# Attention and GLU layer on one core: DMA transposes, LN2 arithmetic on GpSimd, VectorE's exponential tiles planned ahead, and a 512-query chunk split in two

## The chip, the cores and the metric

The kernel runs on one NeuronCore of a Trainium2 chip. Times are device microseconds of that core for one launch, lower being better; the figure of a kernel is the median of its runs. The engines are named as in the profile: PE is TensorE (PEld its weight loads), ACT is ScalarE, DVE is VectorE, POOL is GpSimd, SP is SyncE, which here only issues DMAs. [...]

## The reference

One transformer layer over 2048 tokens of width 640, with 32 heads of 20 and a gated FFN of width 1728, all in bf16:

```python
def _A_ref(x, wqkv, wo):                       # B, S, D = 1, 2048, 640; H = 32, Dh = 20
    qkv = (x @ wqkv).reshape(B, S, 3, H, Dh).transpose(2, 0, 3, 1, 4)
    q, k, v = qkv[0], qkv[1], qkv[2]
    scores = jnp.einsum("bhqd,bhkd->bhqk", q, k) * (Dh ** -0.5)
    p = _softmax(scores, axis=-1)
    o = jnp.einsum("bhqk,bhkd->bhqd", p, v)
    return o.transpose(0, 2, 1, 3).reshape(B, S, D) @ wo

def _B_ref(x, w_gate, w_up, w_down):
    return (_gelu(x @ w_gate) * (x @ w_up)) @ w_down

h  = x + _A_ref(_layernorm(x), A_wqkv, A_wo)
h2 = h + _B_ref(_layernorm(h), B_w_gate, B_w_up, B_w_down)
```

## The kernel before

The program is written as a list of operations (`op`), each with its engine, an estimated duration, a priority (a lower number goes first) and the data that it reads and writes. `Sched.schedule` plays these operations against a small cost model: at every moment each engine takes the ready operation of the best priority for which a PSUM bank is free. The order that comes out is written as a fixed instruction stream for every engine, with semaphore waits. On the chip each engine therefore works strictly in the planned order, and an instruction that is later than planned holds up what the plan put behind it.

The queries are cut in chunks (`SIZES`), seven of them: 512, 512, 256, 256, 256, 128 and 128 rows. They are called chunk 0 to chunk 6 here; by rows, they begin at 0, 512, 1024, 1280, 1536, 1792 and 1920. A chunk is attended in slots of 512 columns (`slots`): one group of four heads times 512 queries, or two groups times 256, or four times 128. There are 32 slots, each with 64 tiles of 128 keys by 512 columns. The score matmuls of a tile (L850) go into PSUM, and the exponential comes next.

Most exponentials run on ACT, in units of three tiles and two tiles in turn (1536 and 1024 columns, banks 0 to 2 and 3 to 4), written to `pts` or to `pts2`, which the profile shows as part of `rege`. Eight tiles of every slot (two in the first) are computed by DVE with integer arithmetic instead (`d_exp`: one read of PSUM per tile at L810, then seven steps on each pair of tiles). The list `dtile` says beside which unit a DVE tile is put; `D_FIRST` and `D_SPAN` spread them over the slot. The product with V (PV, into bank 6) takes DVE tiles at the earliest `D_LAG` = 8 units after they were begun. The last PV of a slot takes all that are left:

```python
while final and d_done:
```

After each slot `epilogue` copies bank 6 to `osb` on DVE, transposes it on PE (L957), and divides into `o_nat` (L966). After a chunk's last slot `post` does the rest. For each tile of 128 rows: `o_nat` is transposed to `oT` on PE (`transposes`, L562) and evicted by DVE (L571), multiplied with `wo` (L614), and added on DVE to the x rows in `h_sb` (L999), which `prefetch` fetched on SP's queue; then come the statistics. For the chunk: `ln_rsqrt` computes the inverse deviation of the second layernorm (LN2) in some 14 small DVE instructions. For each tile again: the normalised row block `xn_t` is written on DVE and transposed to `hnT` (the same buffer as `oT`). Then the FFN: gate matmuls (L1027), copies by DVE (L1056), GELU on ACT in pieces of up to 2048 columns, up matmuls (L1027), products on DVE (L1067), down matmuls (L1078), the last add (L1082) and the output DMA. GELU and the exponential need different tables on ACT; all GELU pieces of a chunk are run together. All of this is background work at priority `P_BG`, between the score matmuls (`P_QK`) and PV (`P_PV`) of the following chunks, in banks 7 and 5.

The last chunk (`tail=True`) has no attention beside it; there the evictions of transposes and the GELU are ACT's, and the square root is too.

Where a chunk's rows lie in `h_sb`, `hnT` and `ha_f` is set by `base`: a chunk of 512 takes all four places of 128 rows; a smaller one takes places 0 and 1, or 2 and 3, by whether its number is even or odd:

```python
return 2 * (c % 2) if CHUNKS[c][1] < 512 else 0
```

PE runs padding matmuls (on `zer` and on `kt_all`) where the plan would leave it idle, so that its clock stays up.

## Time and profile before

| | |
|---|---|
| median of 4 runs | 938.71 us (938.24 to 941.03) |
| the profiled execution, own time | 938.1 us |
| its span (first to last instruction) | 936.4 us |
| granted TensorE clock | 1.00 |
| busy: PE, DVE, ACT, POOL | 857.6, 828.4, 883.5, 12.8 us |
| first exponential begins, last one ends | 35.1, 892.9 us |
| ACT_TABLE_LOAD, all | 14 of 1.28 us |

The profile is of one execution. "Busy" is time in which an engine had an instruction under way; instructions overlap, so the mean duration of one times their number can be more than the busy time. A matmul's end is modelled. The names `rege` and `regw` are two large buffers out of which `h_sb`, `hnT`, `ha_f`, `pts2`, the FFN weights and others are carved; L339 is the line of the helper that records most operations. Attention, by the copies to `osb`, ends at 246.7 us for chunk 0, and then at about 454, 563, 671, 781, 837 and 893.

### The profile page before, as it was taken

The numbers are of one execution on the slowest core, as the hardware profiler recorded it, in microseconds if no ns is written. First come the engines' busy times: TensorE is split into PE (matmuls) and PEld (weight loads), VectorE is DVE, ScalarE is ACT, GpSimd is POOL, SyncE is SP. The second block draws the span as 40 slices with busy tenths as digits, with TensorE's granted clock in tenths as the row PEclk, the third lists the DMA queues.
The fourth block names the chain that finished last, engine by engine and source line by source line (L and its number), as shares of the span: only waits on it lengthen the run. The fifth ranks groups of instructions, "written<-read, shape, count | busy, mean of one in ns | idle before, by whom it ended". The sixth has DMA issues, their size and how long they took to land.

```text
span 936.4 us, 23514 instructions
## 1 busy us (share of the span) xinstructions
PE 857.6 (92%) x10297; PEld 365.1 (39%) x10297; DVE 828.4 (88%) x1807; ACT 883.5 (94%) x799; POOL 12.8 (1%) x33
## 2 busy tenths in 40 slices
PE   3998999999998999998898998999999899999998
PEld 2432222222232222332243333344434546566577
DVE  8859999999899988987799999798999989989953
ACT  7899999999999999999999999999999999999931
POOL 5000000000000000000000000000000000000000
PEclk9999999999999999999999999999999999999999
DMA  7301010322630000001000000000100000000000
GB/s 255 97 19 41 20 49 18 92 62 66 212 110 1 1 2 1 8 15 36 1 2 2 2 1 1 2 2 29 30 2 1 2 27 7 2 17 10 3 22 16
DMA packets 22046, 30.12 MB, mean 32 GB/s; under 512 B 1964, under 2 KB 19464, under 8 KB 21944
## 3 DMA queue, kind: packets, MB, share of 16 engines
q1 hardware_dynamic: 21944, 28.63, 10.0%
q8 instruction: 80, 1.31, 0.6%
q14 instruction: 22, 0.18, 0.1%
HBM read 20.12 MB, written 8.09 MB: 30 GB/s over the span
## 4 chain that ended last, share of the span: by engine, by line
ACT 77%; PE 14%; DVE 8%; issue 1%; DVEq 0%
ACT pts L339 50%; ACT rege L339 26%; PE ps L1027 4%; PE ps L614 3%; PE ps L850 2%; PE ps L1078 2%; PE ps L339 2%; DVE rege L339 2%; DVE qt_all L339 2%; ACT L339 1%; DVE stats L339 1%; DVE rege L810 1%; PE ps L562 1%; DVE qt_all L810 0%; DVE kt_all L339 0%
## 5 line engine op out<-in xcount | busy, mean ns | idle before, releaser
L339 ACT ACTIVATE pts<-ps 128x1536 bf16<-128x1536 f32 x480 | 574.0, 1383 | 6.1 <-PE ps L850 4.3
L850 PE MATMUL ps<-qt_all,kt_all 32*128 32x256 bf16 (+2 forms) x3584 | 303.6, 289 | 42.5 <-ACT pts L339 27.8
L339 ACT ACTIVATE rege<-ps 128x1536 bf16<-128x1536 f32 x239 | 300.7, 1384 | 3.1 <-PE ps L339 3.1
L850 PEld LDWEIGHTS ps<-qt_all,kt_all 32*128 32x128 bf16 x3584 | 95.8, 92 | 275.9 <-ACT pts L339 163.3
L339 DVE TENSOR_TENSOR qt_all<-qt_all 128x1024 bf16<-128x1024 bf16 (+1 forms) x240 | 164.1, 684 | 3.2
L1027 PE MATMUL ps<-rege,regw 128*128 128x256 bf16 (+2 forms) x980 | 152.8, 290 | 9.5 <-ACT rege L339 4.3
L339 PE MATMUL ps<-pts,v_all 128*21 128x256 bf16 (+2 forms) x2098 | 138.8, 290 | 0.5 <-DVE rege L339 0.5
L810 DVE TENSOR_SCALAR rege<-ps 128x512 int16<-128x512 f32 x154 | 105.3, 684 | 27.4 <-PE ps L850 26.5
L339 DVE TENSOR_SCALAR qt_all<-qt_all 128x1024 bf16<-128x1024 int16 (+1 forms) x288 | 115.6, 418 | 2.0
L339 PE MATMUL ps<-rege,v_all 128*21 128x256 bf16 (+2 forms) x1294 | 113.3, 292 | 0.0
L1027 PEld LDWEIGHTS ps<-rege,regw 128*128 128x128 bf16 x980 | 72.8, 97 | 63.5 <-issue 21.2
L614 PE MATMUL ps<-regw 128*128 128x512 bf16 (+1 forms) x360 | 86.3, 349 | 2.0 <-DVE v_all L747 0.7
L1078 PE MATMUL ps<-regw,rege 128*128 128x320 bf16 x448 | 78.0, 301 | 1.9 <-DVE rege L1067 0.8
L810 DVE TENSOR_SCALAR qt_all<-ps 128x512 int16<-128x512 f32 x96 | 65.6, 685 | 3.1 <-PE ps L850 2.2
L339 DVE TENSOR_SCALAR rege<-rege 128x1024 int16<-128x1024 int16 (+2 forms) x166 | 67.1, 420 | 1.1
L339 DVE TENSOR_TENSOR rege<-rege 128x1024 bf16<-128x1024 bf16 (+3 forms) x103 | 65.5, 643 | 0.9
L339 PE MATMUL ps<-kt_all,zer 128*32 128x512 bf16 x740 | 64.8, 385 | 0.0
L339 PEld LDWEIGHTS ps<-pts,v_all 128*21 128x21 bf16 x2098 | 50.2, 91 | 37.2 <-issue 30.8
L1078 PEld LDWEIGHTS ps<-regw,rege 128*128 128x128 bf16 x448 | 36.9, 98 | 32.6 <-issue 15.2
L339 PEld LDWEIGHTS ps<-rege,v_all 128*21 128x21 bf16 x1294 | 41.1, 91 | 19.7 <-issue 13.8
L614 PEld LDWEIGHTS ps<-regw 128*128 128x128 bf16 x360 | 28.4, 98 | 44.7 <-issue 20.2
L1067 DVE TENSOR_TENSOR rege<-rege,ps 128x512 bf16<-128x512 bf16 (+1 forms) x53 | 35.8, 678 | 10.5 <-PE ps L1027 9.7
(92 smaller groups left out, 595.3 us busy)
## 6 DMA issues: line engine op xcount, KB each, us to landing
rege<-in_A_x_dram SPq DMA_DIRECT2D x6, 640.0 KB, 5.1
q_rows<-regw SPq DMA_DIRECT2D x20, 128.0 KB, 1.7
out_dram<-rege SPq DMA_DIRECT2D x16, 160.0 KB, 2.1
regw<-in_B_w_gate_dram SPq DMA_DIRECT2D x1, 2160.0 KB, 12.4
regw<-in_B_w_up_dram SPq DMA_DIRECT2D x1, 2160.0 KB, 17.5
regw<-in_B_w_down_dram SPq DMA_DIRECT2D x1, 2080.0 KB, 22.6
kt_all<-k_rows SPq DMA_DIRECT2D x12, 160.0 KB
qt_all<-q_rows SPq DMA_DIRECT2D x12, 160.0 KB
```

Source lines behind the costliest of these rows:

```text
L339: return lambda eng: getattr(eng, method)(*args, **kwargs)
L562: op("pe", lambda eng, a=a: eng.transpose(bank16(bk, D)[:, 128 * a:128 * a + 128], src[:, a * 128:(a + 1) * 128], ident[:]), 0.055, prio, ...
L614: yield op("pe", lambda eng, l=l, r=r, k=k: eng.matmul(bank(bk, n), l, r, start=(k == 0), stop=(k == len(steps) - 1)), c_mm(n), prio, mode ...
L810: d_ops.append(op("dve", lambda eng: eng.tensor_scalar(v[:, 512 * h:512 * h + 512], bank(b), EXP_MUL, -32000.0, ALU.mult, ALU.max), c_dve( ...
L850: return lambda eng: eng.matmul(out()[:, kk * nq:(kk + 1) * nq], kt_all[32 * j:32 * j + 32, g, kt * 128:(kt + 1) * 128], qt_all[32 * j:32 ...
L1027: op("pe", lambda eng, a=a, f=f, fi=fi: eng.matmul(bank(bk)[:, fi * nq:(fi + 1) * nq], w[:, a, F0[f]:F0[f] + 128], hnT[:, a, 128 * tb:128 ...
L1067: hdone.append(op("dve", lambda eng, bu=bu, fv=fv, w=w: eng.tensor_tensor(fv, fv, bank(bu, w), ALU.mult), c_dve(w), p, reads=[ku, ("ha", k ...
L1078: op("pe", lambda eng, f=f, o=o, hf=hf, bk=bk: eng.matmul(bank(bk, 320), ha_f[:, o:o + 128], wd[:, f, hf * 320:(hf + 1) * 320], start=(f = ...
```

## The change

It has four parts.

- `SIZES` becomes 512, five of 256, and two of 128: the rows 512 to 1023 are two chunks of 256. `base` now counts the chunks of 256 to choose the half, and the last 128 rows take place 3, beside the 128 rows before them in place 2. `ha_f` is divided in quarters to fit, each x fetch has a semaphore of its own, and the wo matmuls wait for the x rows.
- In every chunk but the last, the transposes to `hnT` are done by DMAs issued by SP, and so are those to `oT` in every chunk but the first and the last.
- `ln_rsqrt` of every chunk but the last runs on POOL, but for its reciprocal, which stays on DVE. [...]The work up to xn and its transposes gets the priority `P_LN` = 2.5, ahead of `P_BG` = 3.
- DVE's tiles are first spread over 20 units, not 16, and then each is moved up by as many as `D_LEAD` = 8 units, into the slot before where need be. A DVE tile is taken by a PV of its own slot alone, and one that has waited `D_HOLD` = 4 units beyond its lag gets matmuls of its own in the next PV.

```diff
-SIZES = (512, 512, 256, 256, 256, 128, 128)
+SIZES = (512, 256, 256, 256, 256, 256, 128, 128)
-D_FIRST, D_SPAN = 1, 16
+D_FIRST, D_SPAN, D_LEAD, D_HOLD = 1, 20, 8, 4
-P_QK, P_PV, P_PRO, P_EPI, P_BG = 0, 1, 1.5, 2, 3
+P_QK, P_PV, P_PRO, P_EPI, P_LN, P_BG = 0, 1, 1.5, 2, 2.5, 3
...
-            d = lambda fn, r, w: op("dve", fn, 0.17, prio, reads=r, writes=w)
+            v = lambda fn, r, w: op("dve", fn, 0.17, prio, reads=r, writes=w)
+            d = v if table or sqrt else lambda fn, r, w: op(POOL, fn, 0.25, prio, reads=r, writes=w)
...
-            d(I("tensor_scalar", b.bitcast(I32), a.bitcast(I32), 1, None, ALU.logical_shift_right), ["nw0"], ["nw1"])
-            d(I("tensor_scalar", y.bitcast(I32), b.bitcast(I32), -1.0, RSQRT_MAGIC, ALU.mult, ALU.add), ["nw1"], rk)
+            d(I("tensor_scalar", y.bitcast(I32), a.bitcast(I32), -0.5, RSQRT_MAGIC, ALU.mult, ALU.add), ["nw0"], rk)
             for _ in range(2):
                 d(I("tensor_tensor", b, y, y, ALU.mult), rk, ["nw1"])
-                d(I("scalar_tensor_tensor", out=b, in0=b, scalar=-0.5, in1=a, op0=ALU.mult, op1=ALU.mult),
-                  ["nw0", "nw1"], ["nw1"])
-                d(I("scalar_tensor_tensor", out=y, in0=b, scalar=1.5, in1=y, op0=ALU.add, op1=ALU.mult),
-                  ["nw1"] + rk, rk)
+                d(I("tensor_tensor", b, b, a, ALU.mult), ["nw0", "nw1"], ["nw1"])
+                d(I("tensor_scalar", b, b, -0.5, 1.5, ALU.mult, ALU.add), ["nw1"], ["nw1"])
+                d(I("tensor_tensor", y, y, b, ALU.mult), ["nw1"] + rk, rk)
             d(I("tensor_tensor", sd16[:, t0:t0 + n], a, y, ALU.mult), ["nw0"] + rk, [ks])
-            d(I("reciprocal", y, sd16[:, t0:t0 + n]), [ks], rk)
+            v(I("reciprocal", y, sd16[:, t0:t0 + n]), [ks], rk)
...
+        def dma_transposes(src, rkeys, dst, wkey, after=()):
+            op("sp", I("dma_start_transpose", dst, src), 1.25, P_EPI, reads=rkeys, writes=[wkey], sem=f"xp{wkey[1]}", lat=2.0, after=after)
...
+        dtile = [None] * len(units)
+        u = 0
+        for n, x in dplan:
+            u = max(n - D_LEAD, u, D_FIRST, chunk_u[1] if slots[x[0]][0] == 1 else 0)
+            dtile[u] = x
+            u += 1
...
-                        if u - x_unit[x[2]] >= D_LAG and x[2][3] not in [y[2][3] for y in have]:
+                        if u - x_unit[x[2]] >= D_LAG and x[2][0] == s_ and x[2][3] not in [y[2][3] for y in have]:
                             have.append(x)
                             d_done.remove(x)
-                while final and d_done:
+                if any(x[2][0] == s_ and u - x_unit[x[2]] >= D_LAG + D_HOLD for x in d_done):
                     have = []
...
         def base(c):
-            return 2 * (c % 2) if CHUNKS[c][1] < 512 else 0
+            n = CHUNKS[c][1]
+            if n == 512:
+                return 0
+            half = sum(1 for _, m in CHUNKS[:c] if m == 256) % 2
+            return 2 * half + (n == 128 and CHUNKS[c - 1][1] == 128)
...
-            p = P_EPI if tail else P_BG
+            p = P_EPI if tail else P_LN
...
-                transposes(o_nat[:, tt, :], [("on", g, tt) for g in range(NG)], oT[:, :, tt * 128:(tt + 1) * 128],
-                           ("hnT", tt), banks, P_EPI, ev, after=first)
+                if tail or c == 0:
+                    transposes(o_nat[:, tt, :], [("on", g, tt) for g in range(NG)], oT[:, :, tt * 128:(tt + 1) * 128],
+                               ("hnT", tt), banks, P_EPI, "act" if tail else "dve", after=first)
+                else:
+                    dma_transposes(o_nat[:, tt, :], [("on", g, tt) for g in range(NG)], oT[:, :, tt * 128:(tt + 1) * 128],
+                                   ("hnT", tt), after=first)
...
-                                              for a in range(NA)], [("hnT", tt), "wo"], p))
+                                              for a in range(NA)], [("hnT", tt), "wo"], p, after=(sc.lw[("h", tt, hf)],)))
...
+                if tail:
+                    transposes(xn_t[:, t % 2, :], [("xn", t % 2)], hnT[:, :, tt * 128:(tt + 1) * 128], ("hnT", tt),
+                               banks, p, "act", after=first)
+                else:
+                    dma_transposes(xn_t[:, t % 2, :], [("xn", t % 2)], hnT[:, :, tt * 128:(tt + 1) * 128], ("hnT", tt),
+                                   after=first)
```

## The prediction

> **What bounds the kernel now.** First the page: busy shares, ACT's busy tenths in 40 slices, the chain that ended last.

> ```profile
> PE 857.6 (92%) x10297; PEld 365.1 (39%) x10297; DVE 828.4 (88%) x1807; ACT 883.5 (94%) x799; POOL 12.8 (1%) x33
> ACT  7899999999999999999999999999999999999931
> ...
> ACT 77%; PE 14%; DVE 8%; issue 1%; DVEq 0%
> ```

> ACT is full but for two slices at each end; POOL does nothing after its first memsets. Next the waits: who waited, for whom, us in total, times, longest.

> ```profile
> PEld ps L850 <- ACT pts L339: 163.3, 399, 1.1
> ...
> DVE rege L810 <- PE ps L850: 26.5, 29, 3.5
> ...
> ACT rege L339 <- PE ps L339: 3.1, 2, 1.6
> ...
> ACT pts L339 <- PE ps L339: 1.5, 3, 0.6
> ```

> The score matmuls wait for ACT 399 times, 0.41 us each; ACT hardly waits. In the chain an exponential of 1536 columns and one of 1024 take 2.26 us together, so the 719 take 812 of the 858 us between 35.1 and 892.9. Ten table loads take 13, the GELUs 23; what is left, some 10, is stalls and hand-overs.

> The end is another matter. The last exponential ends at 892.9, the span at 936.4. Timelines of ACT, SP, DVE and PE (start, us, instruction, count, idle before):

> ```profile
> 891.40 1.45 ACT L339 ACTIVATE rege<-ps 128x1536 bf16<-128x1536 f32 x1
> ...
> 904.19 0.34 SPq L339 DMA_DIRECT2D rege<-in_A_x_dram  x1
> ...
> 906.51 0.89 DVE L999 TENSOR_TENSOR rege<-ps,rege 128x320 bf16<-128x320 f32 x2 [0.45 <-DMA rege<-in_A_x_dram]
> ...
> 900.08 1.52 PE L614 MATMUL ps<-wo,rege 128*128 128x320 bf16 x10
> 901.44 6.00 PE L1078 MATMUL ps<-regw,rege 128*128 128x320 bf16 x43
> ...
> 912.01 8.93 PE L1027 MATMUL ps<-rege,regw 128*128 128x128 bf16 x157
> 920.78 3.97 PE L1078 MATMUL ps<-regw,rege 128*128 128x320 bf16 x28
> 924.58 4.52 PE L1027 MATMUL ps<-rege,regw 128*128 128x128 bf16 x78
> 929.62 3.98 PE L1078 MATMUL ps<-regw,rege 128*128 128x320 bf16 x28 [0.52 <-DVE rege L1046]
> ```

> Three chunks' FFN lie in these 43.5 us. The 56 down matmuls up to 907.4 belong to rows 1536-1791, attended by 781; of the 280 gate and up matmuls of 128 columns half, and 28 of the later down matmuls, belong to rows 1792-1919, attended by 837. Only the rest is the last chunk's. And the last chunk's residual add, whose matmuls end at 901.6, waits for its x rows till 906.5: their place in `h_sb` was only freed at 903.7.

> The cause of the lateness is upstream. By the timelines of o_nat, wo and xn_t, chunk 2 (rows 1024-1279) is attended by 563, but its x is fetched at 666.7, when the 512-row chunk 1 leaves `h_sb`, and its first gate matmul starts at 700; rows 1536-1791 need from 781 to 858. Their LN2 instructions run last in priority between DVE's exponential steps (rows 1280-1535 have their wo matmuls before 700 and their xn_t after 730).

> [...]

> **The change part by part.**

> *Split.* No exponential is added: 8 DVE tiles of 64 per slot stay (the last one now falls in unit 19 of 22). One chunk more means one more exp-GELU-exp switch: two loads at 1.30 us (889.18 to the next instruction at 890.48), **+2.6 us on ACT**. GELU columns are the same. PE: 140 matmuls of 512 columns (26 in 5.80 us, 0.223 each, 31.2) become 280 of 256 (13 in 1.59 us, 0.122 each, 34.2): +3 us, under PE's waits for ACT. DVE: two o_nat writes (0.313) for one (0.480) eight times, +1.2. SP: one x fetch more, 0.39.

> *DMA transposes.* 26 of them: one for each of chunk 0's 4 tiles, two for each of 11 others. They take off PE 130 transposes (10 in 0.73 us: 9.5 us) and off DVE 26 evictions at 0.48, 12.5 us; both are beside ACT. They add 26 issues on SP (the planner's 1.25 us each, 33 in all), waiting for o_nat or xn_t; x fetches and outputs queue behind, and SP's own waits show room (398.3 us for DVE's final adds alone). Landing is unknown: the nearest rows (160 KB out 2.1 us, x 2.3) and the planner's 1.25+2.0=3.25 below[...]. I take 3.25; PE, in order, stops if it is more.

> *LN2 on POOL.* 14 small instructions a chunk, 7 chunks. Bounds from POOL's rows: 0.10 us (1x1 memset) to 0.35 (128x160 select). I take 0.30, twice DVE's 0.155: 4.2 us a chunk, against the planner's 0.25 plus about 0.09 of hand-over each, 4.7. DVE loses 13 a chunk, 78 at 0.155, 12 us. [...]nothing on the path while DVE has 108 us idle. The reciprocal on DVE now waits for POOL; exponential steps, FFN evictions and osb copies queue behind it, and PE waits for those banks.

> *Priorities and places.* LN2 and wo now go ahead of FFN work, and 256-row chunks alternate halves of the buffers. Chunk 1's first half can start its FFN when chunk 0's is done (430) instead of after 468, so the backlog is gone before rows 1024-1279 come. Rows 1536-1791 should have gates near 800, not 858, and be done near 870 (chunk 2 needs 65 us, 700 to 765). Rows 1792-1919 follow with gate, GELU and up before 893: their GELU moves off the tail onto ACT, **+4.3** (two switches 2.6, 1.70 for 1792 columns). The last 128 rows get a quarter of their own, so their x is there early.

> *DVE tiles ahead.* Up to 8 units earlier, so the last PV of a slot has fewer left-over quads. Four stalls of ACT end with such a PV (at 92.3, 143.6, 195.3, 323.9: 0.57+1.46+0.38+1.63=4.0). I take **-3.0**; bounds 0 and -7.2, ACT's idle in all stages.

> *The sum.* Last exponential: 892.9+2.6+4.3-3.0=896.8. Tail with the last chunk alone: to the end of wo 8.7 (as now), add 0.5, statistics 0.7, to xn 2.5 (909.07 to 911.59), transposes 1.2, 140 gate and up matmuls at 57 ns 8.0, down 4.0, wait 0.5, last add and output 2.8 (933.6 to 936.4): 28.9. I add 1.0 for the GELU hand-over and 1.0 for what is left of rows 1792-1919: 30.9. Span 927.7, plus the 1.7 between span and own time (938.1): 929.4, or -8.7. The median is 938.7: **930.0 us**.

> **Rivals.**

> *Slower: late DMA transposes.* For: the planner puts their readers on PE as soon as its own figure lets it, and nothing in this trace backs 3.25. Against: 160 KB lands in 2.1 to 2.3. They come in 13 groups; each that lands late by x stops PE, and ACT by x-0.41. [...]It decides at 8.7/13+0.41=1.1 us late, 4.3 from issue to landing. A late POOL chain does the same through the reciprocal: one DVE instruction of 0.68 waited for at every step is 9.5 us a chunk; beyond the 8 units of lag that cover it, a few us, about 945.

> *Little gain.* The backlog stays because DVE (102 of 110 us busy in the stage from 671) limits it: only the wait for x goes, 901.6 to 906.5. 938.7-4.9+2.6=936.4.

> *The FFN of rows 1792-1919 stays in the tail.* Then ACT ends at 892.5, and 12 us of PE work meets 8.8 us of holes in the last chunk's chain: 929 to 931, the same answer.

> *More.* All stalls vanish (4.2 more) and nothing is left of the older rows: 925; with a faster LN2 chain in the tail 922.

> *Not ahead after all.* A tile moved ahead needs bank 7 or 5, which FFN chains hold: -3.0 is lost, 933.

> **How the numbers follow.** The forecast with its neighbours (928 to 933) 0.55, more 0.12, little gain 0.09, the slower rivals 0.20, cancelling ends near the present time 0.04. Within 0.2% (about what a measurement can tell) is 936.8 to 940.6: I put 0.05 there, 0.75 faster, 0.20 slower. The likeliest case's own range is 924 to 935; 8 in 10 need part of the slower case: 917 to 946.

> **What would show it.** Right: fourteen table loads (ten now) between 35 us and the last exponential, ACT idle under 5 us there, the last exponential at 894 to 898, no down matmuls of rows 1536-1791 after it, the last x fetch long before it, L1027 at 128 columns in the tail nearer 140 than 280. Wrong: PE waiting for DMA of oT, hnT or the xn transposes, over 0.5 us each; DVE's reciprocal waiting for POOL; ACT idle over 15 us in attention; or a tail still over 40 us.

## The result, and the profile after

| | before | changed |
|---|---|---|
| median | 938.58 us (937.8 to 941.03, 46 runs) | 935.59 us (928.14 to 941.89, 28 runs) |
| ratio to before | | 0.9971, 95% interval 0.9958 to 0.9984 |
| mean granted TensorE clock, by run | 0.998 to 1.000 | 0.982 to 1.000 |
| profiled execution: span | 936.4 us | 937.5 us, at clock 0.985 |
| last exponential ends, and the tail (from there to the end of the span) | 892.8, 43.6 us | 907.5, 30.0 us |

The change is faster by 0.3%, 3.0 us where 8.7 were forecast. (Three runs of the kernels below, two of "no split" and one of "PE transposes", took over 1.5% longer than the fastest of their kernel and are left out of every figure.) The spread is the first clue: the kernel before repeats within 3 us, the changed one ranges over 14. Over its 28 runs the span follows the clock: a straight line gives 927.6 us plus 0.75 us for each microsecond of clock lost (1 minus the mean clock, times the span), with a correlation of 0.985. The two runs at full clock have spans of 926.4 and 926.9, where 927.7 was forecast.

The page of the changed kernel, profiled at clock 0.985: busy time, ACT's busy tenths, the granted clock, and the chain that ended last.

```profile
PE 870.0 (93%) x11286; PEld 401.5 (43%) x11286; DVE 816.1 (87%) x1712; ACT 892.3 (95%) x803; POOL 38.1 (4%) x131
...
ACT  7889999999997999999999999999999999999991
...
PEclk9999999999997999999999999999999999999999
...
ACT 58%; PE 31%; DVE 7%; DMA 2%; POOL 1%; issue 1%; SPq 0%
```

ACT is now full in all but the last slice, so the tail is shorter, as planned. New is a hole in slice 13 of the ACT row, and the clock has a 7 in the same slice. In the chain ACT has fallen from 77% to 58% and PE has risen from 14% to 31%: more often than before, what ACT does next is released by PE. The waits of the same kernel (who waits, for whom: total us, times, longest):

```profile
PEld ps L857 <- ACT pts L339: 115.2, 312, 1.2
...
DVE rege L817 <- PE ps L857: 44.8, 40, 6.5
...
ACT pts L339 <- PE ps L857: 9.2, 8, 3.7
...
ACT pts L339 <- PE ps L339: 4.3, 3, 1.8
...
ACT rege L339 <- PE ps L857: 4.0, 4, 1.2
```

The scores (L857 here, L850 before) wait for exponentials written to `pts` 312 times, not 399. The other direction has grown: exponentials wait for scores 12 times (8 and 4), together 13.2 us, of which 3.7 are the start of the attention. The kernel before has, the start included:

```profile
ACT pts L339 <- PE ps L850: 4.3, 3, 3.7
```

The tail of the changed kernel, in the timeline of ACT and PE:

```profile
906.04 1.45 ACT L339 ACTIVATE rege<-ps 128x1536 bf16<-128x1536 f32 x1
...
910.32 1.70 ACT L339 ACTIVATE rege<-rege 128x1792 bf16<-128x1792 bf16 x1
...
914.05 3.56 PE L1052 MATMUL ps<-rege,regw 128*128 128x128 bf16 x59
...
918.14 2.89 PE L1109 MATMUL ps<-regw,rege 128*128 128x320 bf16 x20 [0.52 <-DVE sd L339]
...
922.23 7.98 PE L1052 MATMUL ps<-rege,regw 128*128 128x128 bf16 x140
...
930.72 3.98 PE L1109 MATMUL ps<-regw,rege 128*128 128x320 bf16 x28 [0.51 <-DVE rege L1077]
```

Rows 1536 to 1791 are gone from it. The GELU of rows 1792 to 1919 (the activation of 1792 columns) still stands behind the last exponential, with their up matmuls (59 of the 70) and their down matmuls, half of the 56 in the tail. The last line is the end of the last chunk. In all, 217 gate and up matmuls of 128 columns (11, 59, 140 and 7 more) lie behind the last exponential; "What would show it" asked for a number nearer 140 than 280.

Two costs that the trace before could not show, by the DMA issues (median us from issue to landing) and by POOL's timeline of one LN2 chain:

```profile
rege<-xn_t SPq DMA_TRANSPOSE x15, 3.3
...
rege<-o_nat SPq DMA_TRANSPOSE x11, 2.7
```

```profile
439.40 0.19 POOL L339 CAST mv<-mv 128x4 bf16<-128x4 f32 x1 [136.71 <-DVE mv L339]
...
443.43 0.20 POOL L339 TENSOR_TENSOR sd<-nw,rs 128x2 bf16<-128x2 f32 x1
```

This chain takes 4.2 us from 439.40 to 443.63; the seven of the trace take 3.9 to 5.0. Its longest instruction:

```profile
442.70 0.65 POOL L339 TENSOR_TENSOR rs<-rs,nw 128x2 f32<-128x2 f32 x1
```

Its kind takes 0.19 to 0.20 undisturbed. Here a DVE instruction on two SBUF tensors (`TENSOR_TENSOR`) is under way from 442.60 for 0.69 us, and POOL's instruction ends 0.05 us after it. So it is with the other seven POOL instructions of over 0.6 us: each (0.64 to 0.68 us) begins some 0.1 us into such an instruction and ends 0.05 to 0.1 us after it. These DVE instructions hardly lengthen beside POOL (0.691 us in the mean of 9, 0.684 of the other 245). In this trace it is POOL that is held up.

### The profile page after: what moved, and what is told of

The parts are those of the page before. It is cut to its first block, busy times and chain, and to the rows that moved or that the text cites. A ratio compares the mean times of both kernels' runs of the same rounds, so it can differ in the third digit from the quotient of the medians.

```text
span 937.5 us, 25535 instructions
## 1 busy us (share of the span) xinstructions
PE 870.0 (93%) x11286; PEld 401.5 (43%) x11286; DVE 816.1 (87%) x1712; ACT 892.3 (95%) x803; POOL 38.1 (4%) x131
## 4 chain that ended last, share of the span: by engine, by line
ACT 58%; PE 31%; DVE 7%; DMA 2%; POOL 1%; issue 1%; SPq 0%
ACT pts L339 36%; ACT rege L339 20%; PE ps L857 9%; PE ps L339 6%; PE ps L1052 6%; PE ps L616 5%; PE ps L1109 3%; DVE qt_all L339 3%; ACT L339 2%; DMA regw<-in_A_wqkv_dram 1%; DVE rege L817 1%; DVE rege L339 1%; DVE qt_all L817 1%; PE ps L561 1%; POOL nw L339 0%
## 5 line engine op out<-in xcount | busy, mean ns | idle before, releaser
L339 ACT ACTIVATE pts<-ps 128x1536 bf16<-128x1536 f32 x480 | 564.5, 1300 | 14.3 <-PE ps L857 9.2
L857 PE MATMUL ps<-qt_all,kt_all 32*128 32x256 bf16 (+2 forms) x4096 | 339.2, 274 | 28.0 <-ACT pts L339 16.7
L339 ACT ACTIVATE rege<-ps 128x1536 bf16<-128x1536 f32 x239 | 290.5, 1299 | 4.6 <-PE ps L857 4.0
L857 PEld LDWEIGHTS ps<-qt_all,kt_all 32*128 32x128 bf16 x4096 | 121.6, 92 | 244.5 <-ACT pts L339 115.2
L1052 PE MATMUL ps<-rege,regw 128*128 128x256 bf16 (+2 forms) x1120 | 160.0, 276 | 10.0 <-ACT rege L339 6.3
L339 DVE TENSOR_TENSOR qt_all<-qt_all 128x1024 bf16<-128x1024 bf16 (+1 forms) x240 | 164.1, 684 | 4.2
L339 PE MATMUL ps<-pts,v_all 128*21 128x256 bf16 (+2 forms) x2396 | 139.6, 278 | 0.0
L339 DVE TENSOR_SCALAR qt_all<-qt_all 128x1024 bf16<-128x1024 int16 (+1 forms) x288 | 118.7, 418 | 3.7
L339 PE MATMUL ps<-rege,v_all 128*21 128x256 bf16 (+2 forms) x1476 | 114.4, 279 | 0.0
L1052 PEld LDWEIGHTS ps<-rege,regw 128*128 128x128 bf16 x1120 | 85.9, 98 | 64.4 <-issue 32.1
L339 PEld LDWEIGHTS ps<-pts,v_all 128*21 128x21 bf16 x2396 | 59.3, 91 | 38.2 <-issue 30.5
L339 DVE TENSOR_SCALAR rege<-rege 128x1024 int16<-128x1024 int16 (+2 forms) x166 | 68.0, 421 | 1.4
L339 DVE TENSOR_TENSOR rege<-rege 128x1024 bf16<-128x1024 bf16 (+3 forms) x103 | 66.0, 643 | 0.9
L339 PE MATMUL ps<-kt_all,zer 128*32 128x512 bf16 x688 | 57.6, 399 | 0.0
L339 PEld LDWEIGHTS ps<-rege,v_all 128*21 128x21 bf16 x1476 | 46.0, 92 | 17.7 <-issue 13.2
```

What stands on the lines that cost most here:

```text
L339: return lambda eng: getattr(eng, method)(*args, **kwargs)
L857: return lambda eng: eng.matmul(out()[:, kk * nq:(kk + 1) * nq], kt_all[32 * j:32 * j + 32, g, kt * 128:(kt + 1) * 128], qt_all[32 * j:32 ...
L1052: op("pe", lambda eng, a=a, f=f, fi=fi: eng.matmul(bank(bk)[:, fi * nq:(fi + 1) * nq], w[:, a, F0[f]:F0[f] + 128], hnT[:, a, 128 * tb:128 ...
```

## The experiments

Fifteen more kernels were run. The theory at first was: the change does what was forecast, and what is missing is lost clock. The rivals were the sizes and waits of the four parts. The last column of the table takes the lost clock out with the slope found above (span minus 0.75 times the clock lost, mean over the runs); the slope belongs to the changed kernel, so for the others the column, called "at equal clock" below, is an estimate.

| kernel | median, us | ratio to before (95%) | mean clock | span without lost clock, us |
|---|---|---|---|---|
| before | 938.6 | | 0.9998 | 937.1 |
| changed | 935.6 | 0.9971 (0.9958 to 0.9984) | 0.9904 | 927.6 |
| no split | 934.5 | 0.9971 (0.9945 to 0.9998) | 0.9893 | 926.8 |
| LN2 priority as before | 946.3 | 1.0059 (1.0027 to 1.0092) | 0.9866 | 933.3 |
| LN2 on DVE | 940.8 | 1.0031 (1.0013 to 1.0049) | 0.9910 | 933.5 |
| PE transposes | 938.9 | 1.0007 (0.9995 to 1.0019) | 0.9891 | 930.1 |
| no tiles ahead | 935.0 | 0.9966 (0.9956 to 0.9977) | 0.9968 | 931.5 |
| before, with the split | 940.3 | 1.0023 (1.0015 to 1.0030) | 0.9977 | 937.7 |
| before, less padding | 948.7 | 1.0104 (1.0088 to 1.0120) | 0.9757 | |
| changed, more padding | 935.9 | 0.9975 (0.9965 to 0.9985) | 0.9960 | 931.4 |
| scores twice, all borders | 940.7 | 1.0015 (1.0007 to 1.0023) | 0.9959 | 935.7 |
| scores twice, borders up to 345 us | 936.5 | 0.9975 (0.9965 to 0.9985) | 0.9944 | 930.8 |
| the same, no split | 935.9 | 0.9971 (0.9959 to 0.9982) | 0.9951 | 930.7 |
| the same number, mid-slot | 938.9 | 1.0008 (0.9993 to 1.0023) | 0.9944 | 933.8 |
| lulls filled | 932.6 | 0.9939 (0.9927 to 0.9952) | 0.9980 | 929.8 |
| lulls filled, small dose | 934.4 | 0.9950 (0.9936 to 0.9964) | 0.9949 | 928.6 |
| lulls filled, aimed | 931.7 | 0.9927 (0.9913 to 0.9940) | 0.9984 | 929.0 |

### Undoing one part at a time

**The split.** `SIZES` as before, the rest of the change in:

```diff
-SIZES = (512, 256, 256, 256, 256, 256, 128, 128)
+SIZES = (512, 512, 256, 256, 256, 128, 128)
```

> The changed kernel with the second chunk left at 512 rows; DMA transposes, LN2 on POOL, priorities and tiles ahead kept. If the split clears the backlog, as the prediction has it, the backlog is back: rows from 1536 on reach the tail unfinished, the tail after the last exponential is 36 us or more instead of 30, and at an equal clock the time is 4 to 8 us above the changed kernel's. If LN2's priority alone clears it, the tail stays at 30 to 32 us and the time is 2.6 us lower at an equal clock, for two table loads less.

Its tail is 31.2 us, as the second reading had it; at equal clock it is 0.8 us faster than the change, not 2.6. The split does not clear the backlog. Put into the kernel before by itself, it costs 0.6 at equal clock:

```diff
-SIZES = (512, 512, 256, 256, 256, 128, 128)
+SIZES = (512, 256, 256, 256, 256, 256, 128, 128)
-D_PER_SLOT = (8, 8, 8, 8, 8, 8, 8)
+D_PER_SLOT = (8,) * len(SIZES)
```

> The kernel before with the split of its second chunk alone. If the split is what shortens the tail, it is near 34 us (43.5 before) and the time is 932 to 935 us at a full clock. If the priority of LN2 and the faster LN2 chain are needed, the FFN comes as late as before, the tail stays over 40 us and the time is 939 to 942 us, two table loads more. The clock stays at 0.998 or more in both.

The tail there is 39.9 us, and the ratio 1.0023, near what the second reading had. So the split alone is a small loss, and beside the other parts it is worth nothing.

**LN2's priority and engine.** First the priority alone, `P_LN` = 3, then the engine alone (LN2 on DVE, at `P_LN`):

```diff
-P_QK, P_PV, P_PRO, P_EPI, P_LN, P_BG = 0, 1, 1.5, 2, 2.5, 3
+P_QK, P_PV, P_PRO, P_EPI, P_LN, P_BG = 0, 1, 1.5, 2, 3, 3
```

> The changed kernel with the one constant P_LN at 3, the priority of FFN work, as LN2 and wo had before; the order is planned anew. Theory (the priority clears the backlog, not the split): chunks are late again, FFN of rows 1536-1791 in the tail, tail 34 to 43 us, time 938 to 945. Rival (GpSimd and the places in the buffers clear it): tail 30 to 32, 934 to 937 at the same clock as the changed kernel.

```diff
-            d = v if table or sqrt else lambda fn, r, w: op(POOL, fn, 0.25, prio, reads=r, writes=w)
+            d = v
```

> The changed kernel with LN2 on DVE again, at its new priority. If POOL's chain [...]keeps the reciprocal waiting, the time falls by 2 us or more at an equal clock. If it is neutral, the time stays within what its clock explains: 926.4 + 0.75 us for each us of clock lost in the span, plus the 1.7 us around it.

Each is worth about 6 us at equal clock (933.3 and 933.5 against 927.6); of the first, the theory's tail came out, with a median 1.3 us above its range; of the second, neither reading expected a loss. The tail is 34.8 us with the low priority and 38.4 with LN2 on DVE. The priority and the engine do different things. With the low priority 280 gate and up matmuls of 128 columns and 56 down matmuls are left in the tail, with LN2 on DVE 269 and 90 (before 280 and 112, changed 217 and 56). So without the priority, rows 1536 to 1791 are out of the tail all the same, but none of the work on rows 1792 to 1919 is done ahead of it; with LN2 on DVE, 34 down matmuls more are left than the last 256 rows have, so part of rows 1536 to 1791 is still there. It takes both to clear the backlog as far as it is cleared.

**The DMA transposes.** PE transposes everywhere, as before:

```diff
-                if tail or c == 0:
+                if True:
...
-                if tail:
+                if True:
...
-                               banks, p, "act", after=first)
+                               banks, p, "act" if tail else "dve", after=first)
```

> The changed kernel with the 26 DMA transposes made on PE again, evicted by DVE as before. If the removal of 130 PE transposes, which the plan does not count as activity, is what lets the clock fall, it is back at 0.998 or more and the time is 928 to 931 us. If DMA transposes that land late are a cost of their own, the time falls by 2 us or more at an equal clock. If neither, the time is 936 to 939 us with the clock at 0.985 to 0.995, or a little more for DVE's 12 us of evictions.

The third reading held: the clock is lost as in the change, so taking the transposes off PE does not cause that. At equal clock the DMA transposes are worth 2.5 us.

**The tiles ahead.**

```diff
-D_FIRST, D_SPAN, D_LEAD, D_HOLD = 1, 20, 8, 4
+D_FIRST, D_SPAN, D_LEAD, D_HOLD = 1, 16, 0, 4
```

> The changed kernel with DVE's tiles where they were before (D_SPAN 16, D_LEAD 0), the other parts kept. If moving the tiles ahead is what thins PE's work (their matmuls and PV come in bunches), the clock is back to 0.998 or more in most executions and the time is 929 to 933 us, the stalls of ACT at the last PV of a slot being there again (3 us). If it is another part, the clock still falls to 0.985 to 0.995 and the time is 936 to 942 us.

The result lies between the two readings, but this part matters most for the clock: without it the mean clock is 0.9968. At equal clock the tiles ahead are worth 3.9 us (five runs without them at clock 0.998 have spans of 932.2 to 933.3, the changed kernel's one run there 928.9). They lose about as much by the clock, so the median is the same with and without them.

### What the clock costs, and where it goes

Is lost clock costly in the kernel before as well? Its padding was cut:

```diff
-WARM_WIN, WARM_MIN = 3.4, 0.5
-PAD_WIN, PAD_MIN = 3.4, 0.42
+WARM_WIN, WARM_MIN = 3.4, 0.36
+PAD_WIN, PAD_MIN = 3.4, 0.30
```

> The kernel before with less padding: PAD_MIN from 0.42 to 0.30 and WARM_MIN from 0.5 to 0.36. If a thin stretch on PE is enough to halve its clock and that is what costs time, the clock falls below 0.99 and the time rises to 942 us or more, by 0.7 to 0.8 us for each us of clock lost, as over the executions of the changed kernel. If the clock is no cause but a sign, less padding frees PE and the time stays at 936 to 939 us.

The clock falls to 0.973 to 0.978 and the time rises by 10 us. But 23 us of clock are lost here in the mean, so a microsecond of it comes with 0.44 us of time and not with the 0.7 to 0.8 expected. Less padding is also less work for PE, which this run does not tell apart; the slope of the changed kernel cannot be carried over, and the table has no figure there. And can the planner's own padding keep the clock up in the changed kernel?

```diff
-WARM_WIN, WARM_MIN = 3.4, 0.5
-PAD_WIN, PAD_MIN = 3.4, 0.42
+WARM_WIN, WARM_MIN = 3.4, 0.6
+PAD_WIN, PAD_MIN = 3.4, 0.55
```

> The changed kernel with more padding on PE: PAD_MIN from 0.42 to 0.55 and WARM_MIN from 0.5 to 0.6, nothing else. Theory 1 (TensorE's clock): the order of the changed kernel leaves PE with so little work in some stretches that its clock is halved there, and the missing 6 to 8 us are that loss; with more padding the mean clock is 0.998 or more in every execution, the time is 927 to 931 us and its spread is under 2 us. Theory 2 (the clock only follows stalls that the DMA transposes, the POOL chain or the tiles moved ahead make): padding leaves the stalls, the time stays at 934 to 940 us, or rises since PE has more to do.

The spread has shrunk (934.7 to 937.2), but the clock reaches 0.998 only at best, and the padding costs what it saves, some 4 us at equal clock. Neither reading expected both.

All dips of the profiled run begin near a slot border, where the last PV of a slot is done and PE has little but scores. Scores were therefore issued twice there, the second writing the same numbers over the first, in the changed kernel's own order:

```diff
+                if e == "pe" and o.tag and o.tag[0] == "S" and not live:
+                    o.fns = o.fns * 2
                 o.start = t
```

> The changed kernel in exactly its own order; between the last PV of a slot and the first PV of the next, PE issues every score unit's matmuls twice, which writes the same scores again. Theory 1b: the clock is halved because at the borders of slots PE has nothing but the score units and can't be padded there, since padding needs bank 6 with an open sum or bank 7 free, and the last PV has become short. Then the clock is 0.998 or more, the time 927 to 930 us, its spread under 3 us. If the lost clock comes from elsewhere (stalls from DMA transposes, the POOL chain), the clock still falls to 0.985 to 0.995 and the time is 933 to 940 us.

Then the same up to 345 us of the plan only (`and t < 345`), this without the split, and a control in which as many units are doubled ten units later, in the middle of the slots:

```diff
+TWICE = (0,1,2,3,4,5,39,59,60,61,62,82,83,84,104,105,106,127,128,129,149,150,151,171,172,173,194,195,196,216,217,218,219,239,240,261,262,263,283)
...
+                if e == "pe" and o.tag and o.tag[0] == "S" and o.tag[1] in TWICE:
+                    o.fns = o.fns * 2
```

> The changed kernel with its instructions in the same order; the score matmuls between the last PV of a slot and the first PV of the next are issued twice (the second overwrites the first with the same numbers), but only where the order is planned before 345 us, 38 units in all; after that nothing is added. Theory (the clock halves at the slot borders of chunk 0 because TensorE has too little to do there): clock 0.996 or more in every run, spans 927 to 931, time 928 to 932 with the spread of the changed kernel (14 us) gone; no exponential waiting for a score of half speed in 100 to 345. Rival (the clock is lost at random[...]): clock 0.98 to 0.99 as in the changed kernel, or lower, and 935 or more. Second rival (the doubled scores cost as much as the clock they save, as in the run that doubled them in all slots): clock near 1, 936 to 940.

> Chunk 1 of 512 rows in one piece as before, all else of the change in, and the score matmuls at slot borders planned before 345 us issued twice. If the split is worth nothing at equal clock: the same span as with the split and the doubling, within 1.5 us, at a clock of 0.996 or more (927 to 930), unless the border after chunk 1 (500 to 540), which lost clock in the run without the split, loses it again: then up to 934. If the split does clear the backlog: 3 us or more slower than with it at the same clock.

> Control: the changed kernel in its own order, with as many score matmuls issued twice as in the run that doubles them at the borders, but ten units later, in the middle of the slots (the six at the start of the exponentials stay doubled in both). Border theory: the clock is lost as in the changed kernel, 0.98 to 0.995, spans 930 to 938, median near 934 to 936. Rival (any more work on TensorE keeps the clock up, wherever it is): clock 0.996 or more and 928 to 932.

None met its expectation whole. (That the split is worth nothing came out: 930.8 with it and 930.7 without at equal clock.) All four raised the clock to 0.994 to 0.996, the control as much as the borders, and all four cost 3 to 8 us at equal clock. "The borders" was too coarse a cause.

### The window

A dip is a stretch in which the clock stands at half. The grid of the dips gave the answer. In the seventeen traces every dip up to the last matmuls lasts a whole number of times 3.41 us, one to six, and all lie on one grid from the moment when the clock rises. In the changed kernel's trace the clock rises at 18.57 us, and the dips begin at 120.97, 226.78, 277.98 and 363.32, which is 30, 61, 76 and 101 times 3.413 us later; they last one, one, five and one such window. Stretches of this trace on that grid: time, PE, PEld, DVE, ACT and POOL busy, granted clock, DMA share and GB/s.

```profile
core 0: us, PE busy (x) PEld busy (x) DVE busy (x) ACT busy (x) POOL busy (x), PEclk, DMA share, GB/s
...
114.14:117.56 3.42, 3.42 (x25) 0.94 (x24) 3.29 (x7) 3.41 (x4) 0.00 (x0) 1.00 0.11 38
117.56:120.97 3.41, 2.29 (x18) 0.51 (x17) 3.41 (x8) 3.41 (x4) 0.00 (x0) 1.00 0.24 88
120.97:124.38 3.41, 3.37 (x29) 0.85 (x33) 3.41 (x9) 3.04 (x3) 0.00 (x0) 0.50 0.61 139
124.38:127.80 3.42, 2.87 (x39) 0.74 (x31) 2.21 (x6) 2.71 (x4) 0.00 (x0) 1.00 0.13 44
```

One window stands at exactly half clock between two at full clock, and in the window ahead of it PE is not idle, but busy for 2.29 of 3.41 us. Its matmuls, in PE's timeline:

```profile
117.67 0.60 PE L857 MATMUL ps<-qt_all,kt_all 32*128 32x512 bf16 x3
118.21 0.39 PE L339 MATMUL ps<-pts,v_all 128*21 128x512 bf16 x3
118.22 0.39 PE L339 MATMUL ps<-rege,v_all 128*21 128x512 bf16 x1
118.43 0.39 PE L339 MATMUL ps<-pts,v_all 128*21 128x512 bf16 x4
118.75 0.39 PE L857 MATMUL ps<-qt_all,kt_all 32*128 32x512 bf16 x3
119.08 0.39 PE L708 MATMUL ps<-sq,sel 128*32 128x512 bf16 x1
119.67 0.39 PE L857 MATMUL ps<-qt_all,kt_all 32*128 32x512 bf16 x2 [0.20 <-ACT rege L339]
```

Seventeen matmuls, all of 32*128, 128*21 or 128*32, where the largest of these kernels are of 128*128. The planner of the kernel counts 0.213 us of work for 512 columns at 128*128, and a quarter of that, 0.0533, for a matmul of the scores or of PV. With 0.0533 for each of these the work is 17 x 0.0533 = 0.907 us, or **0.27** of the window. The same sum over every full-clock window of all seventeen traces (from five windows after the clock's rise to the last matmul; some records are missing, so it reads a little low):

| work in a window, share | windows | followed by half clock |
|---|---|---|
| under 0.28 | 15 | 15 |
| 0.28 to 0.32 | 25 | 15 |
| 0.32 to 0.36 | 54 | 11 |
| 0.36 to 0.40 | 85 | 1 |
| 0.40 and over | 4190 | 0 |

So in these traces work weighted in this way tells the windows apart: under 0.28 all 15 were followed by half clock, from 0.40 up none of 4190, and between them the share falls, from 15 of 25 to 1 of 85. PE's busy time tells the windows apart far less well: those ahead of half clock have PE busy for 0.40 to 0.87 of the window, and some 760 others under 0.87 were followed by full clock. The kernel before has no window under 0.36 in its trace; the changed kernel has four that are followed by a dip, at 0.27 to 0.31, which begin at 117.6, 223.4, 274.6 and 359.9. In the longest dip the work, by the same sum, is 0.36, 0.30, 0.35, 0.29 and 0.37 in its five windows, so it stays low at half clock, and the clock is full again after the fifth:

```profile
274.57:277.98 3.41, 2.67 (x37) 0.89 (x35) 3.41 (x8) 3.41 (x4) 0.00 (x0) 1.00 0.00 0
277.98:281.39 3.41, 3.06 (x36) 1.41 (x40) 3.41 (x10) 3.41 (x4) 0.00 (x0) 0.50 0.02 5
281.39:284.81 3.42, 3.42 (x41) 1.20 (x33) 1.69 (x4) 1.94 (x3) 0.00 (x0) 0.50 0.00 0
...
291.64:295.05 3.41, 3.41 (x31) 1.27 (x28) 2.34 (x5) 1.97 (x3) 0.00 (x0) 0.50 0.02 5
295.05:298.46 3.41, 3.41 (x53) 1.38 (x49) 3.38 (x10) 3.41 (x4) 0.36 (x2) 1.00 0.00 0
```

In the windows at half clock after 281 ACT is busy for under 2.3 of 3.41 us: this is where the exponentials wait (four times, 1.2 to 1.5 us each, 5.2 in all).

The grid falls differently from trace to trace: the clock's rise, from which it counts, came 18.5 to 21.5 us after the span's start in the seventeen traces. A lull, a stretch with little work, is caught whole by one window or divided between two. This fits the spread: laid over the changed kernel's trace from other beginnings (the long dip left out), the grid has 0 to 5 windows under 0.28, over the trace before none. That the fast runs were those with a lucky grid is argued; only one run of the changed kernel was traced. Sliding a stretch of 3.41 us along a trace from the first exponential on, the places where it can begin and hold under 0.34 add up to 2.6 us before and 24.3 us changed, of which some 7 lie within the long dip, in windows at half clock. Five places go under 0.25 there: beginnings at 117 to 120 (lowest 0.20), 223 to 226 (0.20), 274 to 278 (0.14), 358 to 360 (0.13) and 553 to 554 (0.23), apart from the tail. The last but one and the last lie in GELUs. With borders doubled up to 345 us, 356 to 358 (0.19) and 548 to 552 (0.17) were left, and 280 to 284 (0.25); the control left four of the five. Neither had aimed at the lulls.

**Filling the lulls alone.** By the window theory of the next three runs the clock is lost where a window of the grid falls on a lull and holds less than about a third of work, as the table has it. Fifteen score units (the score matmuls of one exponential each) at these places are issued more than once:

```diff
+TIMES = {72: 2, 73: 2, 74: 2, 161: 2, 162: 2, 163: 2, 206: 2, 207: 3, 208: 3, 209: 3, 210: 2, 272: 2, 273: 5, 430: 2, 431: 5}
...
+                if e == "pe" and o.tag and o.tag[0] == "S":
+                    o.fns = o.fns * TIMES.get(o.tag[1], 1)
                 o.start = t
```

> The changed kernel in its own order; only 15 of its score units are issued more than once: those of the five lulls where, in its trace, some stretch of 3.41 us holds matmul work for under 0.25 of the stretch (work as the planner counts it: 0.213 us for 512 columns, a quarter of that where only 32 rows or columns of the array are used): 117 to 121, 223 to 226, 274 to 284, 358 to 361 and 552 to 555 us. Window theory[...]: clock 0.996 or more in nearly all runs, mean 0.997, spans 927 to 931, median near 930, any dip left in the tail after 905 or at the lulls of which some stretch is still under 0.34. Rival (lulls have nothing to do with it; the clock is lost with chance): mean 0.990, median 935. Second rival (the repeats cost what they save): mean clock 0.997 but 934 to 937.

A smaller dose, `TIMES = {73: 3, 74: 2, 163: 2, 164: 2, 207: 3, 208: 3, 209: 2, 273: 5, 431: 5}`:

> The same with a smaller dose: repeats only on the nine score units that are issued while TensorE would otherwise stand still in the five lulls, none on the units before. Window theory: fewer stretches are lifted over a third, so the mean clock lies between the changed kernel's 0.990 and that of the larger dose, near 0.995; the repeats cost nothing, so spans follow 927 to 928 plus 0.75 us for each us of clock lost: median 930 to 933. Rival (repeats cost as such): the intercept at full clock is 930 or more, as in the kernel with 38 doubled units.

And the large dose, re-aimed by one or two units, `TIMES = {73: 3, 74: 2, 163: 2, 164: 2, 206: 2, 207: 3, 208: 3, 209: 3, 210: 2, 273: 3, 274: 4, 431: 2, 432: 5}`:

> As the larger dose, with the repeats moved by one or two units to where the trace of that run still shows stretches of 3.41 us under 0.34: the units issued during the GELUs at 352 and 545 us (274 and 432 in place of 273 and 431), and only those in the pure lulls at 117 and 223. Nothing is done for the tail's lull at 900 to 903. Window theory: clock 0.998 to 1.000, one window lost at most (in the tail, where little waits for TensorE), spans 927 to 931, median 929 to 932, not slower than the larger dose by over 1 us. Rival (repeats cost as such): 932 to 934 at a clock of 0.998.

The large dose has a clock of 0.998 in each of its five runs; its median of 932.6 misses the expected 930 by 2.6. The small dose has a clock between, as the window theory had it, but its median is 1.4 above the range; its one run at full clock has a span of 927.1, so its repeats, which fall into the lulls, cost little. The aimed dose is the fastest kernel of all, 931.68 us, 0.73% under the kernel before and 3.9 us under the changed one; the intervals of the two ratios lie apart. Its profiled run kept the full clock. The page, and the same lull on this run's grid:

```profile
ACT  6899999999999999999999999999999999999991
...
PEclk9999999999999999999999999999999999999999
...
ACT 63%; PE 27%; DVE 7%; DMA 1%; issue 0%; POOL 0%; SPq 0%
```

```profile
113.64:117.05 3.41, 3.41 (x26) 0.83 (x25) 2.69 (x6) 3.41 (x4) 0.00 (x0) 1.00 0.23 77
117.05:120.46 3.41, 3.41 (x26) 0.94 (x24) 3.38 (x7) 3.40 (x4) 0.00 (x0) 1.00 0.11 38
120.46:123.88 3.42, 2.69 (x30) 0.67 (x27) 3.42 (x8) 3.42 (x4) 0.00 (x0) 1.00 0.43 103
```

The hole in ACT's row is gone, and so are most of its waits for scores, in the waits of this kernel (where L860 is the score line and L342 the helper):

```profile
ACT pts L342 <- PE ps L860: 5.0, 4, 3.7
...
ACT pts L342 <- PE ps L342: 4.3, 3, 1.8
```

Of the 5.0 us, 3.7 are the start of the attention. PE still has 27% of the chain at full clock, so its rise from 14% is for the most part not the clock; the exponentials' short waits below are part of it.

What the three leave open: their spans without lost clock are 928.6 to 929.8, 1 to 2 us above the changed kernel's 927.6, and the aimed kernel's two runs at full clock took 929.8 where the changed kernel's took 926.4 and 926.9. Whether that is a cost of repeats outside the lulls or of where the grid falls was not told apart. The tail's lull (a stretch begun at 900 can hold 0.14) was left as it is.

## Why the prediction was wrong, step by step

**The step that failed is a term that the sum does not have.** "What bounds the kernel now" and "The sum" take the clock of 1.00 as given: PE's work is costed at full speed and put "beside" ACT. The step "DVE tiles ahead" counted only the stalls that a shorter last PV saves; it did not ask whether PE, with a shorter last PV, still has work enough at the slot borders to hold its clock. The changed kernel lost 9.0 us of clock in the mean; at 0.75 that is 6.7 us, and the missing gain is 5.6 (935.6 against 930.0). With the lulls filled 3.9 of them came back. At equal clock the gain is 937.1 - 927.6 = 9.5 us, against 8.7 forecast. That this is so close is in part luck, since several terms are wrong and cancel.

The changed kernel's runs at full clock were not traced. The aimed kernel, at full clock in its profile, stands in for them and shows the terms one by one (before, then aimed); its span is some 3 us longer than theirs:

| term | forecast | measured |
|---|---|---|
| first exponential begins | 0 | +1.6 (35.1, 36.7) |
| table loads up to the last exponential | +2.6, and +4.3 with the GELU of rows 1792 to 1919 | +2.6 (10, 12 loads) |
| ACT's stalls | -3.0 | +0.1 (7.16, 7.23) |
| exponentials and GELUs themselves | 0 | +2.7 |
| tail | -12.6 (43.5, 30.9) | -13.6 (43.6, 30.0) |
| span | -8.7 | -6.6 (936.4, 929.8) |

- *The tail* held in length, 30.0 against 30.9, and in part for the reason given: rows 1536 to 1791 are no longer in it, and the last x rows are there in time. But the sum had the last chunk alone in it, with 1.0 us for the rest, and half of the work on rows 1792 to 1919 is still there (217 matmuls where 140 were the sign). That it fits in the same time is luck.
- *"Split clears the backlog"* ("Priorities and places") failed: the split is worth nothing, and LN2's priority and its engine, each 6 us, do it. The step had named the priority too, but gave the split the credit, and put nothing on the engine.
- *"Their GELU moves off the tail, +4.3"* failed: twelve loads, not the fourteen named as the sign. It is the third rival, which expected about the same total.
- *"DVE tiles ahead, -3.0"*: the four stalls named are gone, but four others that end with a PV stand in their place (1.13 and 1.37 at 65 and 70 us, 0.36 and 1.8 at 262 and 267 in the aimed kernel). Yet the run without this part is 3.9 slower at equal clock: it had one stall of 5.52 at 146. So the tiles ahead are worth what was forecast against the change without them, but not against the kernel before.
- *The 2.7 us of the exponentials* were taken as nothing. They are short waits for scores, which hardly show as idle time. From the end of one exponential to the end of the next, one of 1536 columns takes 1344 ns if it could begin before the one ahead had ended; if its score matmul comes later it loses this overlap, up to 107 ns. In the aimed trace 48 of 359 lost over 20 ns so to a score matmul, 3.7 us together; before it was 13, 1.0 us. Without the tiles ahead it is 16, 1.6 us, so this is a price of the tiles ahead as well, as far as one trace shows.
- *The later start* goes with a later rise of the clock (21.5 us for 18.5) in the aimed run; the changed kernel's trace begins at 35.1, as before.
- *DMA transposes*: 2.7 and 3.3 us to landing in the median, 3.25 taken. PE stopped for one of them once, for 0.8 us, in the changed kernel's trace; the rival of late transposes, put at 4.3 us to landing and over, fell. They are worth 2.5 us at equal clock, which the sum had at nothing, "beside ACT".
- *LN2 on POOL*: 3.9 to 5.0 us a chain, 4.2 taken. DVE was to lose 12 us here and 12.5 of evictions, and to gain 1.2 by the split: -23. The durations of its instructions add up to 913.7 us for 936.8, -23: DVE was not held up, and POOL was, in eight instructions of 0.64 to 0.68 us. (DVE's busy time fell by only 12.3, since its instructions overlap.)
- *"What would show it"* named ACT idle over 15 us in attention as a sign of being wrong, and it was: 15.5 us, in a run at clock 0.985. It stood there beside late DMAs and a late LN2; but 9.5 of the 15.5 are waits for scores, and in the aimed kernel, at full clock, the idle time is 7.2.

The clock as the cause is shown by runs (with the lulls filled, clock and time come back together), and what each part is worth at equal clock by the run without it. That the tiles ahead make the lulls because they leave the last PV of a slot short is argued from the timeline and from the run without them, in whose trace the low stretches come to 10.0 us for 24.3 (about 17 without those inside the long dip).

## What to carry to other kernels

When a change moves TensorE's work about or bunches it, look at its work per window of 3.41 us, weighted as above, before costing anything at full speed: in these traces the windows under 0.28 were followed by half clock 15 times in 15. PE's busy share, 92% before and 93% changed, says nothing of it. If a kernel's time spreads run to run and its mean clock with it, find the dips, and fill those lulls alone with matmuls that nobody waits for: general padding cost what it saved here, and doubling at all borders more. Compare variants at equal clock first, or a part that loses clock is taken for a part that is slow.
